# A decode block on one core: bias columns inside the rows of the first load, and the first load as four loads of stepped partitions

## The chip, the core and the metric

The kernel runs on one core of a Trainium2 chip. The metric is the device time of one execution in microseconds (us). Before the change it is 1050.35 us, the median of three runs from 1050.26 to 1050.51.

## What is computed

One token goes through a transformer block whose two layer norms are shifted, scaled and gated by six vectors that come from a condition `c`: attention of 32 heads over a cache of 8192 positions of 192 elements, and then a dense layer with a squared ReLU. All data are 32-bit floats. Cut to what matters, the reference is:

```python
def reference(A_x, A_k_cache, A_v_cache, A_wq, A_wo, B_x, B_w1, B_b1, B_w2, B_b2, c, w_mod):
    def _A_ref(x, k_cache, v_cache, wq, wo):      # H, Sk, Dh = 32, 8192, 192; D = 640
        q = (x @ wq).reshape(B, Sq, H, Dh).transpose(0, 2, 1, 3)
        scores = jnp.einsum("bhqd,bhkd->bhqk", q, k_cache) * (Dh ** -0.5)
        p = _softmax(scores, axis=-1)
        o = jnp.einsum("bhqk,bhkd->bhqd", p, v_cache)
        return o.transpose(0, 2, 1, 3).reshape(B, Sq, H * Dh) @ wo

    def _B_ref(x, w1, b1, w2, b2):                # F = 1536
        h = x @ w1 + b1
        r = jnp.where(h > 0, h, 0)
        return (r * r) @ w2 + b2

    x = A_x                                       # 1 x 1 x 640
    mod = (_silu(c) @ w_mod).reshape(c.shape[0], 6, 1, -1)
    sa, ca, ga, sb, cb, gb = (mod[:, i] for i in range(6))
    h = _layernorm(x) * (1 + ca) + sa
    x = x + ga * _A_ref(h, A_k_cache, A_v_cache, A_wq, A_wo)
    h = _layernorm(x) * (1 + cb) + sb
    return x + gb * _B_ref(h, B_w1, B_b1, B_w2, B_b2)
```

The caches alone are 2 x 32 x 8192 x 192 x 4 bytes = 403 MB, and each byte is used once.

## The kernel before

**How it is written.** `Program` records the instructions of every engine in the order in which `block_kernel` calls them, works out which semaphores each has to wait for, and `write` (line 139) then emits each engine's stream. So nearly every instruction has line 167 in the profile, and one tells them apart by engine and tile. Waits are found from the ranges of partitions and columns that instructions read and write: `extent` (line 207) gives the range, `overlap` (219) says whether two ranges meet, `within` (223) whether one covers the other. Each load from DRAM (`dma_start` to on-chip memory) takes one of eight semaphores in turn, and waits until the load eight places earlier has landed (lines 104 to 109).

**Loads.** All loads are issued by SP (`nc.sync`), in the order in which they are called. They go into three large buffers called `slot` (line 240) that are used in turn; a load waits until the last readers of its buffer are done. The first buffer takes `first_t`: for each of 128 partitions, a row of `WM` columns of the modulation weights, `WQ` columns of the first query weights, and `VEC` columns of `c` and `x` (33,320 bytes in all). Line 244 loads it in one piece. Then come the K block of head 0 (k0, line 350) and in the loop over heads (line 476) the V block of head 0 (v0), the four small loads of the bias vectors into a tile `bbc` of its own (lines 485 to 488, cut into 8, 4, 12 and 104 partitions by `BB_CUT`), and from then on a K and a V block for each head in turn. `kx` rows also carry slices of the query and output weights for later heads. k1 goes into the buffer of `first_t`, v1 into that of k0, and so on. After the last head SP loads the weights of the dense part (lines 517 to 531).

**The start.** ACT and DVE compute silu of `c` (lines 352 to 356); DVE weighs the modulation weights (`weigh`, line 334) while the layer norm of `x` runs beside it; TensorE sums over partitions and then forms the first two heads' query (`query`, line 371, called at 381). Then `spread` (line 293) turns the columns of `x` into rows: ACT copies each column 32 times into a tile `spread`, of which there is one buffer, and DVE transposes that to `x_t` (line 382). The biases get the same treatment at head 3 (line 490), into `bbt`; `bbt` is used only in the dense part (lines 569 and 581).

**One head.** `keys` (line 386) multiplies the K block with the query on DVE, and sums over the 192 elements on DVE, with GpSimd adding halves of some. `softmax` and `values` follow; TensorE multiplies with the V block. The query of the next pair of heads is formed from the tail of a K row.

Of the kernel before, what the change touches and what calls it, by code (L numbers as in the profile page):

```python
# [1 line left out]

# [9 lines left out]
P = 128  # L12
D = 640
# [7 lines left out]
KB = DG // 32  # L21
FB = FG // 32
# [5 lines left out]
WQ = KB * PW  # L28
ROW = KV + WO
WM = KB * 2 * D  # L30
VEC = 2 * KB
DA = 128
DB = DH - DA
REP = 8
# [2 lines left out]
WO_AT = {2 * i + 4: i for i in range(-1, NPAIR - 2)} | {H - 1: NPAIR - 2}  # L37
WQ_AT = {2 * i + 1: i + 1 for i in range(NPAIR - 1)}
WIDE = {h for h, i in (WO_AT | WQ_AT).items() if i >= 0}
BB_CUT = (8, 4, 12, 104)  # L40
HALF = DG // 2
W2_CUT = (0, 6 * D, 9 * D, 11 * D, 11 * D + G * HALF, FB * D)
EPS = 1e-5
# [7 lines left out]
class Program:  # L51
# [43 lines left out]
    def record(self, engine, name, args, kwargs):  # L95
# [14 lines left out]
        else:  # L110
            self.ticks[engine] += 1
            mark = (engine, self.ticks[engine])
        places = [(extent(a), w) for a, w in [(a, False) for a in reads] + [(a, True) for a in writes] if a.space != MemoryType.DRAM]
        for place, write in places:
            for other, who, wrote in self.uses.get(place[0], ()):
# [91 lines left out]
def extent(ap):  # L207
    row = ap.tensor.shape[1]
    (step, n), *free = ap.ap
    p, lo = divmod(ap.offset, row)  # L210
    hi = lo + sum((c - 1) * s for s, c in free) + 1
    end = p + (n - 1) * (step // row) + 1
    bank = ap.space == MemoryType.PSUM
    if bank:
        p, end, lo, hi = p // 32 * 32, -(-end // 32) * 32, lo // 512 * 512, -(-hi // 512) * 512
    return ap.tensor.name, p, end, lo, hi, bank


def overlap(a, b):
    return a[1] < b[2] and b[1] < a[2] and a[3] < b[4] and b[3] < a[4]  # L220


def within(a, b):
    return b[1] <= a[1] and a[2] <= b[2] and b[3] <= a[3] and a[4] <= b[4]


def block_kernel(nc, first, kx, vx, wm1, w1, w2, bb, out):
    def const(shape, name):
        return nc.tile(shape, name)

    def work(shape, tag, bufs=2):
        return nc.tile(shape, tag, bufs)
# [6 lines left out]
    def slot():  # L239
        return nc.tile([P, ROW], "slot", 3, align=512)  # L240

    k_t, v_t = {}, {}
    first_t = slot()
    nc.sync.dma_start(first_t[:, :WM + WQ + VEC], first)

    ident = const([P, P], "ident")
    make_identity(nc, ident)
# [12 lines left out]
                            axis=AX.X, op=ALU.add)  # L260
# [3 lines left out]
                            axis=AX.X, op=ALU.add)  # L264
# [5 lines left out]

    vec = first_t[:, WM + WQ:WM + WQ + VEC]
    c_c = vec[:, :KB]
    x_c = vec[:, KB:2 * KB]
    bbc = const([P, FB + KB], "bbc")

    def load_k(h):
        k_t[h] = slot()
        n = K_PARTS.get(h, 1)
        cuts = [KV * c // n for c in range(n)] + [ROW if h in WIDE else KV]
        for a, b in zip(cuts, cuts[1:]):  # L280
            nc.sync.dma_start(k_t[h][:, a:b], kx[h, :, a:b])

    def load_v(h):
        v_t[h] = slot()
        nc.sync.dma_start(v_t[h][:, :KV], vx[h])
# [7 lines left out]
    def spread(src, n, name):  # L293

        t = work([P, FB + KB, 32], "spread", 1)
        nc.scalar.copy(t[:, :n], src[:, :, None].to_broadcast([P, n, 32]))
        r = const([P, 32 * n], name)
        nc.vector.transpose(r, t[:, :n].rearrange("p b r -> p (b r)"))
        return r

    def total(src, name):

        ps = psum("sm")
        n = src.shape[1]
        nc.tensor.matmul(ps[:, :n], ones, src, start=True, stop=True)
        return ps[:, :n]
# [35 lines left out]
    def attend(i, w, oT):  # L342

        nc.fresh = True
        for j in range(3):
            for g in range(G):
                nc.tensor.matmul(att[32 * g:32 * (g + 1), :DG], oT[:, j:j + 1].to_broadcast([P, 32]),
                                 w[:, j, DG * g:DG * (g + 1)], start=False, stop=(i == NPAIR - 1 and j == 2))
# [24 lines left out]
    def query(i, w):  # L373
        w = w.rearrange("p (b n) -> p b n", b=KB)
        ps = psum("q", at=0)
        for b in range(KB):
            nc.tensor.matmul(ps[:, :PW], h1[:, b:b + 1].to_broadcast([P, P]), w[:, b], start=(b == 0), stop=(b == KB - 1))
        qb_t[i] = work([P, PW], "qb")
        nc.scalar.activation(qb_t[i], ps[:, :PW], AF.Copy, scale=DH ** -0.5)

    query(0, first_t[:, WM:WM + WQ])
    x_t = spread(x_c, KB, "x_t")

    ri_t, o_t, sp_t, os_t, sum_t, m_t, pt_t = {}, {}, {}, {}, {}, {}, {}

    def keys(h, between):

        q = qb_t[h // 2][:, DH * (h % 2):DH * (h % 2 + 1)]
        sc = work([P, NPOS], "sc")
        t = k_t[h][:, :KV].rearrange("p (i d) -> p i d", d=DH)  # L390
        sums = SUMS.get(h, ((32, 0),))
        n = NPOS // len(sums)
        for c, (nf, na) in enumerate(sums):
            a, b = n - nf - na, n - na
            pr = t[:, c * n:(c + 1) * n]
            s = sc[:, c * n:(c + 1) * n]
            nc.vector.tensor_mul(pr, pr, q[:, None, :].to_broadcast([P, n, DH]))
            nc.gpsimd.tensor_add(pr[:, a:b, :DH // 2], pr[:, a:b, :DH // 2], pr[:, a:b, DH // 2:])
            for i in range(b, n):
                jk = work([P, DH], "jk")  # L400
                nc.scalar.activation(jk, pr[:, i], AF.Copy, accum_out=s[:, i:i + 1])
            nc.vector.tensor_reduce(s[:, :a], pr[:, :a], axis=AX.X, op=ALU.add)
            if c == 0:
                between()
            nc.vector.tensor_reduce(s[:, a:b], pr[:, a:b, :DH // 2], axis=AX.X, op=ALU.add)
        return sc

    def softmax(h, sc):
        mp = work([P, 1], "mp")
        nc.vector.tensor_reduce(mp, sc, axis=AX.X, op=ALU.max)  # L410
        ps = psum("sm")
        nc.tensor.transpose(ps[:, :P], mp.to_broadcast([P, P]), ident)
        nm = work([P, 1], "nm")
        nc.vector.tensor_reduce(nm, ps[:, :P], axis=AX.X, op=ALU.max, negate=True)

        p = work([P, NPOS, REP], "p", 1)
        i = h // 2
        if h % 2 == 0:
            sp_t[i] = work([P, 2], "sp", 3)
        nc.scalar.activation(p, sc[:, :, None].to_broadcast([P, NPOS, REP]), AF.Exp, bias=nm,  # L420
                             accum_out=sp_t[i][:, h % 2:h % 2 + 1])
        return p
# [17 lines left out]
    def own(h, after=None):  # L440

        i, a = h // 2, h % 2
        if not a:
            m_t[i] = work([P, 2, 1024], "own", 1)
            os_t[i] = work([P, P], "os", 3).rearrange("p (a d) -> p a d", a=2)
        if i not in ri_t and (a or i == NPAIR - 1):
            ri_t[i] = work([P, 2], "ri", 3)
            nc.vector.reciprocal(ri_t[i], sum_t.pop(i))
        m, o = m_t[i][:, a], o_t.pop(h)
        cuts = (0, 512, 1024) if h == H - 1 else (0, 1024)  # L450
        for lo, hi in zip(cuts, cuts[1:]):
            nc.vector.tensor_mul(m[:, lo:hi], o[:, lo:hi], mask[:, lo:hi], after=after)
        if i == NPAIR - 1:
            nc.vector.tensor_reduce(os_t[i][:, a], m[:, 512:].rearrange("p (j d) -> p d j", d=DB), axis=AX.X, op=ALU.add)
        elif a:
            nc.vector.tensor_reduce(os_t[i], m_t[i][:, :, 512:].rearrange("p a (j d) -> p a d j", d=DB), axis=AX.X, op=ALU.add)
# [19 lines left out]
    for h in range(H):  # L476
        i = h // 2
        if h % TURN == 1 and (h < H - 1 or nc.turns):
            nc.loop(h < H - 1)
        if h:  # L480
            load_k(h)
        load_v(h)
        if h == 0:
            nc.gpsimd.memset(v_t[0][:, KV:ROW], 0.0)
            r0 = 0
            for n in BB_CUT:
                nc.sync.dma_start(bbc[r0:r0 + n], bb[r0:r0 + n])
                r0 += n
        if h == 3:
            bbt = spread(bbc, FB + KB, "bbt")  # L490

        def wo():
            if h in WO_AT:
                attend(WO_AT[h], k_t[h][:, KV:ROW].rearrange("p (j n) -> p j n", j=3), oT_t.pop(WO_AT[h]))

        def between():
            if h in WQ_AT:
                query(WQ_AT[h], k_t[h][:, KV:ROW])
            if h < H - 1:
                wo()  # L500

        sc = keys(h, between)
        p = softmax(h, sc)
        if h == H - 1:
            sum_t[i] = total(sp_t.pop(i), f"sum{i}")
            wo()
        if h:
            own(h - 1, qb_t.get(h // 2 + 1))
        if h % 2 == 0 and h:
            turn(i - 1)  # L510
        if h == H - 1:
            turn(i, (0,))
        values(h, p)
        if h % 2 and h < H - 1:
            sum_t[i] = total(sp_t.pop(i), f"sum{i}")
# [132 lines left out]
```

## Time and profile before

| | before |
|---|---|
| median of 3 runs | 1050.35 us (1050.26 to 1050.51) |
| the profiled execution | 1050.38 us |
| its span, first to last instruction | 1049.1 us |
| read from DRAM | 451.82 MB, 431 GB/s over the span |
| DVE busy | 829.3 us (79%) |
| PE busy | 457.0 us (44%) |
| POOL busy | 213.3 us (20%) |
| ACT busy | 69.0 us (7%) |
| load queue, share of 16 DMA engines | 99.6% |

PE is TensorE, DVE is VectorE, ACT is ScalarE, POOL is GpSimd, and SP issues the loads. Busy time of an engine is the sum of its instructions; the DMA share is the busy share of the core's 16 DMA engines. The span is what the profiler saw of the execution; the device time holds a little more around it.

### The profile page before, as it was taken

The numbers are of one execution on the slowest core, as the hardware profiler recorded it, in microseconds if no ns is written. First come the engines' busy times: TensorE is split into PE (matmuls) and PEld (weight loads), VectorE is DVE, ScalarE is ACT, GpSimd is POOL, SyncE is SP. The second block draws the span as 40 slices with busy tenths as digits, with TensorE's granted clock in tenths as the row PEclk, the third lists the DMA queues.
The fourth block names the chain that finished last, engine by engine and source line by source line (L and its number), as shares of the span: only waits on it lengthen the run. The fifth ranks groups of instructions, "written<-read, shape, count | busy, mean of one in ns | idle before, by whom it ended". The sixth has DMA issues, their size and how long they took to land. (4 is left out here: it accounts for less than half of the span.)

```text
span 1049.1 us, 6398 instructions
## 1 busy us (share of the span) xinstructions
PE 457.0 (44%) x2736; PEld 207.5 (20%) x2736; DVE 829.3 (79%) x284; ACT 69.0 (7%) x247; POOL 213.3 (20%) x50
## 2 busy tenths in 40 slices
PE   1153452535445064453526355163443516353456
PEld 0011221112122031222203122121212103121223
DVE  6788778988787987878888787897878798778852
ACT  1000000000000000000000000000000000012330
POOL 1221122221122221022222022222012222022100
PEclk9666665766657576675666658566665766666569
DMA  9999999999999999999999999999999999999998
GB/s 403 446 429 430 419 448 433 422 448 431 430 427 437 445 424 440 435 435 429 428 446 431 431 426 444 437 427 437 437 430 427 435 444 433 428 440 435 428 424 357
DMA packets 11266, 451.99 MB, mean 431 GB/s; under 512 B 1525, under 2 KB 1781, under 8 KB 2037
## 3 DMA queue, kind: packets, MB, share of 16 engines
q1 hardware_dynamic: 11253, 451.83, 99.6%
q8 instruction: 7, 0.11, 0.0%
q14 instruction: 6, 0.05, 0.0%
HBM read 451.82 MB, written 0.00 MB: 431 GB/s over the span
## 5 line engine op out<-in xcount | busy, mean ns | idle before, releaser
L167 DVE TENSOR_TENSOR slot<-slot,qb 128x12288 f32<-128x12288 f32 (+2 forms) x37 | 415.3, 11225 | 133.3 <-DMA slot<-in_kx 133.3
L167 POOL TENSOR_TENSOR slot<-slot 128x3072 f32<-128x3072 f32 (+2 forms) x37 | 210.3, 5683 | 791.6 <-DVE slot L167 791.6
L167 DVE TENSOR_REDUCE sc<-slot 128x32 f32<-128x6144 f32 (+5 forms) x74 | 307.0, 4150 | 13.3 <-POOL slot L167 12.0
L167 PE MATMUL ps_o<-slot,p 128*32 128x512 f32 x1536 | 240.8, 791 | 22.2 <-PEq L161 21.0
L167 PE MATMUL ps_q<-slot,ln_h 128*128 128x384 f32 x160 | 88.9, 728 | 80.6 <-PEq L161 79.3
L167 PE MATMUL ps_sm<-ident,mp 128*128 128x128 f32 x32 | 14.0, 438 | 248.9 <-PEq L161 213.0
L167 PEld LDWEIGHTS ps_o<-slot,p 128*32 128x32 f32 x1536 | 63.4, 140 | 175.3 <-issue 171.6
L167 PE MATMUL ps_q<-slot,oT 128*32 128x160 f32 x408 | 29.5, 453 | 154.6 <-PEq L161 154.4
L167 PEld LDWEIGHTS ps_q<-slot,ln_h 128*128 128x128 f32 x160 | 45.4, 296 | 128.5 <-issue 122.7
L167 PEld LDWEIGHTS ps_sm<-ident,mp 128*128 128x128 f32 x32 | 5.7, 179 | 267.3 <-issue 229.9
L167 ACT ACTIVATE p<-sc,nm 128x512 f32<-128x512 f32 x32 | 23.1, 721 | 525.7 <-DVE nm L167 525.7
L167 PE MATMUL ps_sm<-ri,own 128*128 128x1 f32 x256 | 56.5, 350 | 0.0
L167 PEld LDWEIGHTS ps_sm<-ri,own 128*128 128x128 f32 x256 | 55.0, 326 | 0.2
L167 PEld LDWEIGHTS ps_q<-slot,oT 128*32 128x32 f32 x408 | 18.2, 158 | 158.1 <-issue 155.2
L167 DVE TENSOR_TENSOR own<-ps_o,mask 128x1024 f32<-128x1024 f32 (+1 forms) x33 | 38.9, 1178 | 9.5 <-PE ps_o L167 9.5
L167 DVE TENSOR_REDUCE os<-own 128x128 f32<-128x1024 f32 (+1 forms) x17 | 30.2, 1774 | 0.6
L167 PE MATMUL ps_sm<-ri,os 128*64 128x1 f32 x64 | 6.4, 247 | 55.1 <-POOLq L165 54.4
L167 DVE TENSOR_REDUCE nm<-ps_sm 128x1 f32<-128x128 f32 x32 | 9.3, 292 | 21.2 <-PE ps_sm L167 21.2
L167 ACT ACTIVATE jk<-slot 128x192 f32<-128x192 f32 x69 | 24.0, 349 | 32.0 <-DVE slot L167 32.0
L167 ACT ACTIVATE qb<-ps_q 128x384 f32<-128x384 f32 x16 | 7.8, 490 | 272.8 <-PE ps_q L167 272.8
L167 PEld LDWEIGHTS ps_sm<-ri,os 128*64 128x64 f32 x64 | 5.3, 203 | 60.4 <-issue 58.4
L167 ACT ACTIVATION_READ_ACCUMULATOR jk<-slot 128x1 f32 x69 | 12.9, 187 | 0.0
(81 smaller groups left out, 93.4 us busy)
## 6 DMA issues: line engine op xcount, KB each, us to landing
slot<-in_kx SPq DMA_DIRECT2D x28, 7104.0 KB, 28.1
slot<-in_vx SPq DMA_DIRECT2D x32, 6144.0 KB, 22.6
slot<-in_kx SPq DMA_DIRECT2D x2, 6144.0 KB, 25.4
slot<-in_kx SPq DMA_DIRECT2D x2, 4032.0 KB, 23.8
slot<-in_kx SPq DMA_DIRECT2D x2, 3072.0 KB, 16.9
slot<-in_first SPq DMA_DIRECT2D x1, 4165.0 KB, 12.5
slot<-in_wm SPq DMA_DIRECT2D x1, 3840.0 KB, 25.5
slot<-in_w SPq DMA_DIRECT2D x1, 3840.0 KB, 31.8
```

The lines of the kernel that those rows point to most:

```text
L167: i = getattr(engine, name)(*args, **kwargs)
```

## The change

The bias columns are put into the rows of `first`, behind `c` and `x`: `VEC` grows from 10 to 27 columns, the array `bb`, its tile and its four loads go, and `bbc` becomes a view of `first_t`. The spread of the biases to `bbt` is called right after that of `x`, ahead of the first head, and no longer at head 3. The first load is issued as four: partitions 0, 8, 16, .. (16 of them), then 4, 12, 20, .. (16), then 2, 6, 10, .. (32), then the odd ones (64). So that these loads don't wait for each other, `extent` also gives the step of the partitions, `overlap` uses it (two ranges meet only if their starts agree modulo the common divisor of the steps), and `within` holds only where the covering range has no step.

```diff
-VEC = 2 * KB
+VEC = 3 * KB + FB
+FIRST_CUT = ((0, 8), (4, 8), (2, 4), (1, 2))
...
-BB_CUT = (8, 4, 12, 104)
...
-    return ap.tensor.name, p, end, lo, hi, bank
+    return ap.tensor.name, p, end, lo, hi, bank, 1 if bank else max(step // row, 1)
 
 
 def overlap(a, b):
-    return a[1] < b[2] and b[1] < a[2] and a[3] < b[4] and b[3] < a[4]
+    return a[1] < b[2] and b[1] < a[2] and a[3] < b[4] and b[3] < a[4] and (a[1] - b[1]) % gcd(a[6], b[6]) == 0
 
 
 def within(a, b):
-    return b[1] <= a[1] and a[2] <= b[2] and b[3] <= a[3] and a[4] <= b[4]
+    return b[6] == 1 and b[1] <= a[1] and a[2] <= b[2] and b[3] <= a[3] and a[4] <= b[4]
...
-    nc.sync.dma_start(first_t[:, :WM + WQ + VEC], first)
+    for r, step in FIRST_CUT:
+        nc.sync.dma_start(first_t[r::step, :WM + WQ + VEC], first[r::step])
...
-    bbc = const([P, FB + KB], "bbc")
+    bbc = vec[:, 2 * KB:]
...
     x_t = spread(x_c, KB, "x_t")
+    bbt = spread(bbc, FB + KB, "bbt")
...
-            r0 = 0
-            for n in BB_CUT:
-                nc.sync.dma_start(bbc[r0:r0 + n], bb[r0:r0 + n])
-                r0 += n
-        if h == 3:
-            bbt = spread(bbc, FB + KB, "bbt")
...
-        "first": np.concatenate([rows(wm[:, :2 * D], KB), wq[0], column(c, KB), column(a(A_x).ravel()[order], KB)], axis=1),
+        "first": np.concatenate([rows(wm[:, :2 * D], KB), wq[0], column(c, KB), column(a(A_x).ravel()[order], KB),
+                                 column(B_b1, FB), column(a(B_b2)[order], KB)], axis=1),
...
-        "bb": np.concatenate([column(B_b1, FB), column(a(B_b2)[order], KB)], axis=1),
```

## Rows read from the trace of the kernel before

**Rows 1.** The page: span, busy time, DMA over the run, load queue, HBM.

```profile
span 1049.1 us, 6398 instructions
PE 457.0 (44%) x2736; PEld 207.5 (20%) x2736; DVE 829.3 (79%) x284; ACT 69.0 (7%) x247; POOL 213.3 (20%) x50
...
DMA  9999999999999999999999999999999999999998
...
q1 hardware_dynamic: 11253, 451.83, 99.6%
...
HBM read 451.82 MB, written 0.00 MB: 431 GB/s over the span
```

**Rows 2.** Windows view, middle of the run; columns in the first line.

```profile
core 0: us, PE busy (x) PEld busy (x) DVE busy (x) ACT busy (x) POOL busy (x), PEclk, DMA share, GB/s
13.00:1000.00 987.00, 426.09 (x2381) 191.92 (x2381) 804.57 (x249) 58.86 (x208) 208.41 (x36) 0.65 1.00 434
```

**Rows 3.** Chain that ended last, its end: start us, us, what.

```profile
1020.41 25.14 DMA slot<-in_w
1045.55 0.04 issue
1045.59 1.17 PE ps_q L167 x32
```

**Rows 4.** Windows view, start of the stream and start of k1's rows.

```profile
0.00:1.70 1.70, 0.00 (x0) 0.00 (x0) 0.00 (x0) 0.97 (x1) 0.85 (x7) 1.00 0.00 0
1.70:2.60 0.90, 0.00 (x0) 0.00 (x0) 0.52 (x1) 0.31 (x1) 0.84 (x6) 1.00 1.76 444
2.60:3.60 1.00, 0.00 (x0) 0.00 (x0) 1.00 (x1) 0.00 (x0) 1.00 (x1) 1.00 0.35 133
3.60:4.60 1.00, 0.00 (x0) 0.00 (x0) 1.00 (x1) 0.00 (x0) 0.36 (x1) 1.00 1.24 533
12.30:13.00 0.70, 0.00 (x0) 0.00 (x0) 0.00 (x0) 0.00 (x0) 0.00 (x0) 1.00 2.61 1124
41.30:42.10 0.80, 0.00 (x0) 0.00 (x0) 0.80 (x1) 0.00 (x0) 0.00 (x0) 0.50 2.78 1148
```

**Rows 5.** Timeline of SP, first issues: start us, us, what.

```profile
0.74 0.38 SPq L167 DMA_DIRECT2D slot<-in_first  x1
1.18 0.42 SPq L167 DMA_DIRECT2D slot<-in_kx  x1
1.65 0.42 SPq L167 DMA_DIRECT2D slot<-in_vx  x1
2.11 1.77 SPq L167 DMA_DIRECT2D bbc<-in_bb  x4
31.24 0.36 SPq L167 DMA_DIRECT2D slot<-in_kx  x1
```

**Rows 6.** DMA view of the window 41.30:42.10.

```profile
DMA packets 197, 0.92 MB, mean 1148 GB/s; under 512 B 181, under 2 KB 181, under 8 KB 181
```

**Rows 7.** The page, DMA issues: count, KB each, us from issue to landing.

```profile
slot<-in_first SPq DMA_DIRECT2D x1, 4165.0 KB, 12.5
```

**Rows 8.** Timeline about head 3: the bias spread.

```profile
119.77 0.64 ACT L167 COPY spread<-bbc 128x544 f32<-128x544 f32 x1
120.45 0.74 DVE L167 STREAM_TRANSPOSE bbt<-spread 128x544 f32<-128x544 f32 x1 [4.93 <-ACT spread L167]
```

**Rows 9.** Timeline of the first two heads.

```profile
30.90 0.32 ACT L167 COPY spread<-slot 128x160 f32<-128x160 f32 x1
31.23 1.28 ACT L167 ACT_TABLE_LOAD   x1
...
31.25 0.35 DVE L167 STREAM_TRANSPOSE x_t<-spread 128x160 f32<-128x160 f32 x1 [6.82 <-ACT spread L167]
31.51 12.92 DVE L167 TENSOR_TENSOR slot<-slot,qb 128x12288 f32<-128x12288 f32 x1
...
54.61 0.35 SPq L167 DMA_DIRECT2D slot<-in_vx  x1
...
59.11 12.96 DVE L167 TENSOR_TENSOR slot<-slot,qb 128x12288 f32<-128x12288 f32 x1 [3.42 <-DMA slot<-in_kx]
```

**Rows 10.** Windows view, before and at the start of v1's rows.

```profile
57.30:58.10 0.80, 0.80 (x8) 0.20 (x4) 0.00 (x0) 0.00 (x0) 0.00 (x0) 0.50 0.00 0
58.10:58.90 0.80, 0.80 (x8) 0.20 (x4) 0.00 (x0) 0.00 (x0) 0.00 (x0) 0.50 2.28 983
```

**Rows 11.** Windows view, end of the stream.

```profile
1043.00:1044.00 1.00, 0.63 (x20) 0.30 (x11) 0.00 (x0) 0.00 (x0) 0.00 (x0) 1.00 0.99 401
1044.00:1045.00 1.00, 1.00 (x24) 0.68 (x24) 0.00 (x0) 0.00 (x0) 0.00 (x0) 1.00 0.69 270
1045.00:1046.00 1.00, 0.43 (x16) 0.40 (x16) 0.00 (x0) 0.00 (x0) 0.00 (x0) 1.00 0.45 159
```

More of the change, by code (lines that the diff above doesn't have):

```diff
@@ L1 @@
-from math import prod
+from math import gcd, prod
 from concourse import mybir
@@ L215, in extent, with block_kernel @@
         p, end, lo, hi = p // 32 * 32, -(-end // 32) * 32, lo // 512 * 512, -(-hi // 512) * 512
-    return ap.tensor.name, p, end, lo, hi, bank
+    return ap.tensor.name, p, end, lo, hi, bank, 1 if bank else max(step // row, 1)
 def overlap(a, b):
-    return a[1] < b[2] and b[1] < a[2] and a[3] < b[4] and b[3] < a[4]
+    return a[1] < b[2] and b[1] < a[2] and a[3] < b[4] and b[3] < a[4] and (a[1] - b[1]) % gcd(a[6], b[6]) == 0
 def within(a, b):
-    return b[1] <= a[1] and a[2] <= b[2] and b[3] <= a[3] and a[4] <= b[4]
-def block_kernel(nc, first, kx, vx, wm1, w1, w2, bb, out):
+    return b[6] == 1 and b[1] <= a[1] and a[2] <= b[2] and b[3] <= a[3] and a[4] <= b[4]
+def block_kernel(nc, first, kx, vx, wm1, w1, w2, out):
     def const(shape, name):
```

## Prediction

> **What bounds the kernel now.** I read the page first, then the chain of work that ended last, then windows of the run, and then the first 60 us as a timeline. On the page the reader is to see that the load queue is busy for 99.6% of the span, that the DMA row stands at 9 in all slices but the last, and that 452 MB come in at 431 GB/s [rows 1]. VectorE is busy for 79% of the span and waits again and again for the next K block; no compute engine is the bound. The window over 987 us in the middle gives a DMA share of 1.00 at 434 GB/s [rows 2], that is 434/16 = 27.1 GB/s for each of 16 DMA engines. The chain that ended last says the same of the end: 25.14 us of it is the last weight loads, and behind them come 1.17 us of matmul, the small VectorE work on `y` and the store, issued at 1047.57 of a span of 1049.1 [rows 3]. So the time is: 1.7 us until the first packet moves (no DMA in 0.00:1.70 [rows 4]), the stream until about 1046, and some 3 us of tail. A change at the head counts in full if it delays or shortens the stream, and for nothing if it only moves compute in front of a load that is waited for anyway.
>
> **The base of the sum.** The profiled execution took 1050.38 us for a span of 1049.1, so 1.3 us lie around the span; it is 0.03 above the median of 1050.35. The sum starts from 1050.38.
>
> **The bias loads go.** Four loads of 0.3 to 6.9 KB are removed. On SP they cost 1.77 us from 2.11 on [rows 5], and SP's next instruction, the load of k1, then waits until 31.24 for the first buffer; so their issue time costs nothing. In the stream they lie between v0 and k1. All 181 packets under 512 B that start in 41.30:42.10 (128 bias rows, the rest semaphore writes) fit into that 0.8 us, in which k1's first rows start as well [rows 6, 4]. If the small ones took the whole window the gain would be 0.8 us; the window also holds 0.91 MB in packets that start there, so the engines were not held up for that long. I take -0.1, bounds -0.8 and 0. The same bytes now ride in the first load, 68 B more on a row of 33,320: 0.2% of 9.8 us, +0.02.
>
> **Three more issues at the head.** The first load was one issue of 0.38 us; k0's and v0's followed at 1.18 and 1.65 [rows 5]. Four issues of about 0.44 us move k0's to about 2.5. What hides that is the first load itself: k0's rows start in 12.30:13.00 (1124 GB/s for 0.7 us are 787 KB, 16 rows of 49,152 B; the view books a packet where it starts [rows 4]). Cover left: over 8 us. Cost 0; without the cover it would be 1.3 us. Nothing else is on SP between them. The first stepped load gives each engine one row of 1.23 us, and the next issue comes 0.44 us later, so no engine runs dry between the four. Three more sets of semaphore writes: +0.03, by the same small packets.
>
> **The start of the stream.** In 1.70:2.60 there start 0.9 us x 444 GB/s = 400 KB, 12 rows; in 2.60:3.60 133 KB, 4 rows; in 3.60:4.60 533 KB, 16 rows [rows 4]. So twelve engines begin about 1.0 us after the issue at 0.74 and four about 0.9 us later. A load of 16 rows may let the four start with the rest: at most -0.9. But all sixteen start their second row within the same 1 us, so the four made most of it up already. I take -0.1, bounds -0.9 and 0.
>
> **The rate of the stepped loads** is the term that decides, and no row shows it. 4165 KB [rows 7] are 4.265 MB; at 434 GB/s that is 9.83 us, 1.23 us for each of an engine's 8 rows. One bound is that they run like the first load of before, the nearest row: +0. The other is that a step of 8 partitions sends the engines two and two to one place of the on-chip memory while other places stand idle; each row then takes twice as long: +9.83. Every large load of the kernel covers all 128 partitions in one piece, and those that don't are the bias loads of 8.5 KB together, whose rate can't be read. I take +0 because the nearest row, the same bytes from the same array to the same tile, runs at full rate; the other end stays in the range. [...]
>
> **The bias spread moves from head 3 to the start.** It is an ACT copy of 0.64 us and a DVE transpose of 0.74 [rows 8]. Both spreads share one buffer, so the copy waits for the transpose of `x_t`, which ends at 31.60, and the large multiply of k0 behind it on DVE starts not at 31.51 [rows 9] but at 31.60 + 0.03 + 0.64 + 0.03 + 0.74 = 33.04: +1.53 on DVE's path. SP's k1 load, which waits for the last reader of the first buffer, moves from 31.24 to about 32.3; v0 runs until 41.3, so 8 us of cover hide it. Tighter is v1: its load was issued at 54.61 [rows 9], when k0 was used up, and goes to 56.14. Its first packets then come 1.0 us later, or 1.9 for the slow four: 57.1 to 58.1. No packet starts in 57.30:58.10, and sixteen rows start in 58.10:58.90 [rows 10]: the engines turn to v1 only after 58.1, since k1 lasts until then. So the move just fits, with 0 to 1.0 us left. I take +0. Upper bound: if ACT's table load of 1.28 us [rows 9] came between the two copies, v1's packets would be 0.2 to 1.2 us late, +1.2. Behind that the delay dies: DVE waited 3.42 us for k1 at 59.11 [rows 9]. At head 3 DVE no longer sits 4.93 us [rows 8] before the transpose; what comes next there is again a wait for a load, so that is worth 0.
>
> **Sum:** 1050.38 - 0.1 + 0.02 + 0.03 - 0.1 = 1050.2.
>
> **The end of the stream** adds scatter. The DMA share falls over 1043 to 1046 as 0.99, 0.69, 0.45 [rows 11]: the engines finish over some 2 us, and the last one sets the time. The bias loads were cut in four unequal pieces, so they weigh unevenly on the engines, and a new start shifts them too; 0.31 + 0.55 = 0.86 us is what perfect balance would gain. I allow 0.8 down and 0.8 up.
>
> **Rivals.** (A) *The stepped loads run at half rate throughout.* Two engines that share a place finish together and meet again at the next row, all 8 rows long. Price 8 x 1.23 = 9.8 us, all of it on the stream: 1060.0. For it: the stream's rate is the same over 987 us, for arrays with different row lengths in DRAM, so the limit sits behind the source, in the engine or at the place where it writes. Against it: if the limit is the engine's own, the order of partitions is nothing to it. It decides from the first row on which two engines meet. (B) *Only part of it.* If just the two loads of 16 rows meet, that is 2 x 1.23 = 2.5 us, 1052.7; if one of each pair gets ahead by a row and they no longer meet, 1.2 us, 1051.4. (C) *v1 comes late*, in the place of the hidden spread: up to +1.2, 1051.4; against it the 0 to 1.0 us that are left. (D) *Faster in earnest.* Over 2.1 us would need more than the whole 1.7 us ahead of the first packet. (E) *The four loads do not start the late engines earlier*, so that the change does only the moves that are hidden: 1050.3, within the forecast.
>
> **How the numbers follow.** A measurement of this kernel can tell about 0.2%, 2.1 us, from no change. Forecast 1050.2, with (C) and (E), own range 1049.4 to 1051.4: chance 0.54. (A), 1058.5 to 1061: 0.30. (B), 1051.4 to 1055: 0.14, of which a little over half is beyond 2.1 us. (D): 0.02. So faster 0.02, same 0.60, slower 0.38. To hold 8 in 10 the range has to reach into (A): 1049.4 to 1060.5.
>
> **What would show it.** In the windows at the head, the stepped loads right at full rate: sixteen rows start by 2.6, k0's rows start by 12.3 to 13.0 again, and ACT's first work on `c` stands near 13.3. Under (A) k0 starts near 22 and ACT near 23; under (B) near 14 to 15 and 15 to 16. The multiply of k0 should start 1.5 us later behind the first landing than before, 19.8 instead of 18.3 us behind it, and a window just ahead of v1's first rows should show a DMA share that does not sag; if it sags, (C). The DMA share in the middle stays 1.00. I am wrong if the stream's length from the first packet to 1046 changes by more than 1 us though the head windows look like before.

## The result and the profile after

The changed kernel takes 1054.36 us, the median of six runs from 1054.14 to 1054.85. Against the runs of the kernel before it is slower by a factor of 1.0037, with a 95% interval of 1.0027 to 1.0047. That is 4.0 us more, where 1050.2 had been forecast.

The page of the changed kernel shows the stream as full as before, only longer:

```profile
span 1053.0 us, 6394 instructions
...
DMA  9999999999999999999999999999999999999998
...
q1 hardware_dynamic: 11136, 451.83, 99.5%
...
HBM read 451.82 MB, written 0.00 MB: 429 GB/s over the span
```

The end of the chain that ended last (start us, us, what) has the same steps with nearly the same lengths (the last matmuls 1.21 us in place of 1.17). They start at 1049.51 in place of 1045.59 [rows 3], so all 3.9 us are lost ahead of the tail:

```profile
1049.46 0.04 issue
1049.51 1.21 PE ps_q L167 x32
1050.72 0.02 issue
```

Where they are lost is seen in windows of the changed kernel (last two columns: share of the DMA engines and GB/s; a packet's bytes are booked where it starts, so GB/s times the length, divided by the row, counts the rows that start):

```profile
core 0: us, PE busy (x) PEld busy (x) DVE busy (x) ACT busy (x) POOL busy (x), PEclk, DMA share, GB/s
1.70:2.60 0.90, 0.00 (x0) 0.00 (x0) 0.52 (x1) 0.00 (x0) 0.84 (x6) 1.00 2.51 556
2.60:3.60 1.00, 0.00 (x0) 0.00 (x0) 1.00 (x1) 0.00 (x0) 1.00 (x1) 1.00 0.13 33
3.60:6.40 2.80, 0.56 (x8) 0.23 (x8) 2.80 (x2) 0.00 (x0) 0.36 (x1) 1.00 0.86 191
8.30:14.50 6.20, 0.00 (x0) 0.00 (x0) 0.87 (x1) 0.00 (x0) 0.00 (x0) 1.00 1.00 431
14.50:15.30 0.80, 0.00 (x0) 0.00 (x0) 0.00 (x0) 0.00 (x0) 0.00 (x0) 1.00 2.28 983
...
60.30:61.20 0.90, 0.00 (x0) 0.00 (x0) 0.29 (x1) 0.57 (x1) 0.00 (x0) 0.50 2.30 710
61.20:61.90 0.70, 0.41 (x4) 0.20 (x8) 0.45 (x1) 0.24 (x2) 0.00 (x0) 0.50 0.64 211
```

**The first loss, 2.3 us.** By 2.60, 15 rows of 33,388 B have started and one more by 3.60. Then 16 rows (535 KB) start from 3.60 to 6.40, and the third set only after that: the engine that is first through its two rows needs 4.3 us for them, from 2.1 on. By the trace's packet records the rows of the two loads of 16 partitions take 2.39 and 2.40 us in the mean, the next ones 1.63, and all that follow 1.24 (8.30 to 14.50 runs at 431 GB/s). The first row of each engine was slow before the change too: 1.93 us in the mean, and 1.24 or less from the second on. So, in means over the sixteen engines, the loss is 0.23 us from the later first packets, 0.45 and 1.16 from the two loads of 16, and 0.39 from the third set. Sixteen rows of k0 start in 14.50:15.30, where they started in 12.30:13.00 before [rows 4].

**The second loss, 1.6 us.** v1's sixteen first rows started together in 58.10:58.90 before [rows 10]. Moved by the first loss they would start between 60.3 and 61.1. Thirteen do so by 61.20 and three only in 61.20:61.90. The stretch from k1's first row to k2's first row holds the same bytes in both kernels, 435 GB/s over 31.2 us and 423 over 32.1. The windows view of the kernel before:

```profile
41.40:72.60 31.20, 7.95 (x50) 2.25 (x51) 26.90 (x7) 0.81 (x2) 7.13 (x2) 0.61 1.01 435
```

The same view of the changed kernel, its stretch 0.9 us longer:

```profile
43.50:75.60 32.10, 9.38 (x51) 2.75 (x52) 30.36 (x7) 0.81 (x2) 7.79 (x2) 0.61 1.00 423
```

That is 0.9 us for the first engine; for the last one, by the packet records, v1's rows end at 77.2 in place of 73.3, 3.9 us later, so 1.6 us behind the first loss of 2.3. The slowest engine sets the end of the stream, and the 3.9 us are found again at the last matmuls. In the profiled executions of all eleven changed versions, the last of v1's rows and the whole span are late by the same time to 0.2 us, but for `e9_packed_source` (2.63 and 2.98) and `e1_bias_only` (1.73 and 2.37).

The packet records also show what this loss consists of. Ahead of v1's first rows the engines stand idle for 0.26 us in the mean; these rows then take 2.51 us in the mean, where they took 1.81 before. So most of the loss is in slow first rows, and the idle time is the smaller part.

Why v1 was late is seen in the timelines (start us, us, what, idle time ahead and its releaser). In the kernel before, ACT has loaded its table ahead of its wait for the first load:

```profile
0.73 1.28 ACT L167 ACT_TABLE_LOAD   x1 [0.73 <-PEq L640]
13.30 0.21 ACT L167 ACTIVATE silu<-slot 128x5 f32<-128x5 f32 x1 [11.29 <-DMA slot<-in_first]
```

In the changed kernel it does so behind that wait:

```profile
0.73 2.52 SPq L167 DMA_DIRECT2D slot<-in_first  x4
...
15.87 1.28 ACT L167 ACT_TABLE_LOAD   x1 [15.87 <-DMA slot<-in_first]
17.17 0.21 ACT L167 ACTIVATE silu<-slot 128x5 f32<-128x5 f32 x1
...
34.69 0.34 DVE L167 STREAM_TRANSPOSE x_t<-spread 128x160 f32<-128x160 f32 x1 [6.39 <-ACT spread L167]
35.07 0.64 ACT L167 COPY spread<-slot 128x544 f32<-128x544 f32 x1 [0.41 <-DVE x_t L167]
...
35.74 0.74 DVE L167 STREAM_TRANSPOSE bbt<-spread 128x544 f32<-128x544 f32 x1 [0.71 <-ACT spread L167]
36.41 12.92 DVE L167 TENSOR_TENSOR slot<-slot,qb 128x12288 f32<-128x12288 f32 x1
...
59.51 0.33 SPq L167 DMA_DIRECT2D slot<-in_vx  x1
```

k0's multiply starts 4.90 us later than before (36.41 and 31.51 [rows 9]), and so does the issue of v1 (59.51 and 54.61). The stream itself was only 2.3 us late. The 4.90 us are: the landing of the first load, at which ACT leaves its wait (15.87 in place of 13.30, +2.57); a table load of ACT that now stands behind that wait (+1.30); the bias spread behind that of `x` (+1.46: from the start of the transpose to `x_t` to k0's multiply it is 1.72 us in place of 0.26); less 0.42 us, by which the query's matmuls were shorter (5.57 us in place of 5.99).

### The profile page after: what moved, and what is told of

Its sections match the earlier page's. It is cut to its first block, busy times and chain, and to the rows that moved or that the text cites. A ratio compares the mean times of both kernels' runs of the same rounds, so it can differ in the third digit from the quotient of the medians.

```text
span 1053.0 us, 6394 instructions
## 1 busy us (share of the span) xinstructions
PE 458.9 (44%) x2736; PEld 208.3 (20%) x2736; DVE 829.3 (79%) x284; ACT 69.0 (7%) x247; POOL 213.3 (20%) x50
```

## Experiments

**The theory** after the comparison: two separate losses. The two loads of 16 partitions run at half rate (2.39 and 2.40 us a row, where 1.24 is the full rate); the loads of 32 and 64 do not (1.63 us, then 1.24). And what piles up ahead of k0's multiply (late landing, table load, bias spread) makes v1 late. That two engines each meet at one place of the on-chip memory in the loads of 16 is a supposition; the traces show times alone. **The rivals:** all of the loss is in the stepped loads; the first rows are slow because the stream starts with small loads, or because there are four of them; the step is slow on DRAM's side. All medians stand against 1050.44 to 1050.46 of the kernel before on the same chips.

### One part at a time

`e1_bias_only`, the changed kernel with the first load in one piece:

```diff
-    for r, step in FIRST_CUT:
-        nc.sync.dma_start(first_t[r::step, :WM + WQ + VEC], first[r::step])
+    nc.sync.dma_start(first_t[:, :WM + WQ + VEC], first)
```

> The bias columns ride in the rows of the first load, which is one load again; the bias spread stays ahead of head 0. Theory: the 4 us of the change are two pieces, about 2.3 us from the stepped loads of 16 partitions (their rows take 2.40 us in place of 1.23) and about 1.6 us from v1's load, which comes late because the bias spread, a table load of ACT and the late landing pile up ahead of k0's multiply. With one load the landing is at 13.2 again and the table load ahead of it, so only the spread's 1.5 us are left ahead of v1's issue (56.1 in place of 54.6), v1's packets come between 57.1 and 58.2, just in time: 1050.3, between 1050.0 and 1050.9. Rival (the spread alone makes v1 late): a gap of 1 us and more ahead of v1's rows, 1051.4 to 1052.

Measured: 1050.77 (ratio 1.0006, 0.9997 to 1.0016), but runs from 1050.3 to 1053.7. So this version stands on the edge that the prediction had worked out, with 0 to 1.0 us left for v1. The profiled execution took 1052.76 and fell over it: v1 was issued at 56.83, and of its sixteen first rows 12 (655 GB/s for 0.9 us) start by 58.90 and 4 only in the next 1.2 us:

```profile
58.00:58.90 0.90, 0.09 (x4) 0.09 (x8) 0.00 (x0) 0.76 (x2) 0.00 (x0) 0.50 1.88 655
58.90:60.10 1.20, 1.20 (x8) 0.32 (x12) 0.75 (x1) 0.00 (x0) 0.00 (x0) 0.50 0.53 164
```

`e2_steps_only`, the four stepped loads, with the bias in its own loads again and spread at head 3:

```diff
-VEC = 3 * KB + FB
+VEC = 2 * KB
...
-    bbt = spread(bbc, FB + KB, "bbt")
...
+        if h == 3:
+            bbt = spread(bbc, FB + KB, "bbt")
```

> The first load as four stepped loads, but the bias in its own four loads and spread at head 3, as in the kernel before. Theory: the stream is 2.3 us late from k0 on; k0's multiply starts 2.6 + 1.3 us later (late landing, table load behind it), so v1's issue is at about 58.5 and its packets at 59.5 to 60.4, as the engines run out of k1 at about 60.4: at most a small gap, 1052.7, between 1052.4 and 1053.3. Rival (all of the loss is in the stepped loads, the gap at v1 is a by-product): 1054.3.

Measured: 1052.90 (1.0023, 1.0014 to 1.0033), as the theory said. The steps alone cost 2.5 us and the bias alone 0.3, together 2.8 of the 4.0: by the medians the two parts hurt each other by 1.2 us. Each ratio's interval is about 1 us to either side, so the 0.3 can't be told from nothing, and the 1.2 is rough.

### What is slow about the stepped loads

`e3_reversed`, the same four loads in reverse order:

```diff
-FIRST_CUT = ((0, 8), (4, 8), (2, 4), (1, 2))
+FIRST_CUT = ((1, 2), (2, 4), (4, 8), (0, 8))
```

> The changed kernel with the four stepped loads in reverse order: the odd partitions (64), then 2, 6, .. (32), then 4, 12, .. (16), then 0, 8, .. (16). Theory (two engines meet at one place of the on-chip memory in a load of 16 stepped partitions): six rows of 1.24 us first, then two of 2.40; the windows show a full rate up to about 9 us and about half of it (16 rows in 2.4 us, some 220 GB/s) in the 4.8 us ahead of k0, which starts near 14.5; total as the changed kernel within 0.5 us, 1053.8 to 1054.8. Rival (the first rows are slow because the stream starts with small loads, whichever partitions they hold): full rate at the end, k0 near 12.6, and 1052 to 1052.5.

Measured: 1055.56 (four runs, 1055.19 to 1056.16). The slow rows moved to the end with the two loads of 16, so they are not slow because they stand at the start of the stream. (The very first rows are slow here too, 1.86 us in the mean, as in the kernel before.) Windows of this kernel:

```profile
2.00:10.10 8.10, 0.76 (x8) 0.23 (x8) 7.09 (x2) 0.00 (x0) 1.96 (x6) 1.00 1.00 396
10.10:14.30 4.20, 0.00 (x0) 0.00 (x0) 0.00 (x0) 0.00 (x0) 0.00 (x0) 1.00 1.07 254
```

The last 32 rows (254 GB/s x 4.2 us = 1.07 MB) take 4.2 us; by the packet records they take 2.10 and 2.39 us each. The total is 0.8 us above the range given: here the landing, and with it v1's issue (61.38), are later still than in the changed kernel, while k0's first row starts at about the same time (14.4), so the gap at v1 is wider: by the packet records the engines stand idle ahead of it for 1.39 us in the mean, in place of 0.26.

`e4_four_of_32`, as many loads, but of 32 partitions:

```diff
-FIRST_CUT = ((0, 8), (4, 8), (2, 4), (1, 2))
+FIRST_CUT = ((0, 4), (1, 4), (2, 4), (3, 4))
```

> The changed kernel with four stepped loads of 32 partitions each (step 4, starting at 0, 1, 2, 3): as many issues and semaphores, no load of 16. Theory: no row takes 2.4 us, k0's rows start near 12.7 (the stepped issue takes 0.2 us longer), so 1.9 us of the 2.3 come back; what is left is the gap at v1, since table load and spread are still ahead of k0's multiply: 1052.4, between 1052.0 and 1052.9. Rival (four pieces in place of one cost it, whatever their rows): k0 again near 14.6 and 1054.3.

Measured: 1052.25 (1.0016, 1.0007 to 1.0026), as the theory said. k0's sixteen first rows start in 12.60:13.20 (1311 GB/s), so four stepped loads without one of 16 cost the stream 0.3 us:

```profile
2.00:12.60 10.60, 0.76 (x8) 0.23 (x8) 7.08 (x2) 0.00 (x0) 1.96 (x6) 1.00 1.01 403
12.60:13.20 0.60, 0.00 (x0) 0.00 (x0) 0.00 (x0) 0.00 (x0) 0.00 (x0) 1.00 3.04 1311
```

`e6_contiguous`, as many rows in each load as the change has, without a step:

```diff
-    for r, step in FIRST_CUT:
-        nc.sync.dma_start(first_t[r::step, :WM + WQ + VEC], first[r::step])
+    for lo, hi in ((0, 16), (16, 32), (32, 64), (64, 128)):
+        nc.sync.dma_start(first_t[lo:hi, :WM + WQ + VEC], first[lo:hi])
```

> The changed kernel with the first load cut into partitions 0 to 15, 16 to 31, 32 to 63 and 64 to 127, no step. Theory (a load gets only the share of the write places that its partitions reach, and neighbours lie in one place): four engines meet in the first two loads, two in the others; rows of 4.9, 4.9, 2 x 2.45 and 4 x 2.45 us, the first load takes some 24.5 us in place of 9.9, and the total is 1050.4 + 14.7 + up to 2 for a late v1: 1065 to 1067. Rival (it is the step that costs, in the load's description or in DRAM): rows of 1.24 us, and 1052.3 as with four loads of 32.

Measured: 1065.93 (two runs). Neighbouring partitions are far worse than stepped ones, so the step itself is not the cause. The first load takes until 25.9, at 177 GB/s; k0's first rows start only then:

```profile
1.70:25.90 24.20, 0.76 (x8) 0.23 (x8) 7.09 (x2) 0.00 (x0) 2.21 (x6) 1.00 1.01 177
25.90:26.60 0.70, 0.00 (x0) 0.00 (x0) 0.00 (x0) 0.00 (x0) 0.00 (x0) 1.00 3.26 1124
```

The theory fits in the sum: its counts and the 1.23 us of a row gave 24.5 us, and from the first packet at 1.7 it measured 24.2. How many engines meet was assumed; the packet records show times alone. The single rows fit less well than the sum: 3.74 and 4.55 us in the mean for the two loads of 16, where 4.9 had been expected, and 2.47 to 3.17 for the other six sets, where 2.45 had been. This run also answers a rival of its own: a load of 16 has just one row for each of the 16 engines, in steps of 8 as well as here, and the rows differ all the same (2.40 and 4.55 us). So the set of partitions counts, and not only the small number of rows. A third set of 16 partitions, neither in steps of 8 nor neighbours, was not run.

`e9_packed_source`, the array `first` laid out in DRAM in the order in which the four loads take its rows, so that only the destination is stepped:

```diff
+    lo = 0
...
-        nc.sync.dma_start(first_t[r::step, :WM + WQ + VEC], first[r::step])
+        nc.sync.dma_start(first_t[r::step, :WM + WQ + VEC], first[lo:lo + P // step])
+        lo += P // step
...
```

> The changed kernel with the rows of the first array in the order in which the four loads take them, so that each load reads one packed piece of DRAM and only the destination is stepped. Theory (the destination decides): rows of the first two loads at 2.40 us as before, 1053.8 to 1054.9. Rival (the stepped read of DRAM is slow): full rate, k0 near 12.7, 1052.3.

Measured: 1053.45 (five runs), a little below the range given and far above the rival's. The rows of the two loads of 16 stay slow: 32 rows (248 GB/s x 4.3 us) start by 6.30, and the rest runs at 438:

```profile
2.00:6.30 4.30, 0.46 (x8) 0.23 (x8) 4.21 (x2) 0.00 (x0) 1.96 (x6) 1.00 1.04 248
8.20:14.30 6.10, 0.00 (x0) 0.00 (x0) 1.00 (x1) 0.00 (x0) 0.00 (x0) 1.00 1.02 438
```

So the stepped read is not what makes the rows slow; what is left is the destination. Here the landing came 0.6 us earlier than in the changed kernel, and the gap at v1 was narrower; whether the packed read is behind that, five runs don't settle.

### The late v1

`e5_early_table`, one Exp of one column on ACT ahead of its wait for the first load:

```diff
     nc.gpsimd.memset(eps_t, EPS)
+    nc.scalar.activation(const([P, 1], "warm_exp"), eps_t, AF.Exp)
```

> The changed kernel with one small Exp on ACT ahead of its wait for the first load, so that ACT's table load is done at the start and not behind the landing. Theory: everything on the way to v1's issue moves 1.3 us up, v1's issue to 58.2, its packets to 59.2 to 60.4; the engines run out of k1 from 60.3 on, so the gap all but closes and 1.0 to 1.6 of the 4.0 us come back: 1053.0, between 1052.6 and 1053.4. Rival (the gap at v1 costs nothing of its own): 1054.3.

Measured: 1052.86 (1.0029, 1.0018 to 1.0039). 1.5 of the 4.0 us come back by moving a table load that is not on the stream at all: v1 is issued at 58.32, and five of nine runs lie at 1052.6 to 1052.9; single ones reach 1055.5. That this version is on the edge again would explain them, but no trace shows such a run.

`e8_after_spread_first`, both spreads ahead of the first query:

```diff
+    x_t = spread(x_c, KB, "x_t")
+    bbt = spread(bbc, FB + KB, "bbt")
     query(0, first_t[:, WM:WM + WQ])
-    x_t = spread(x_c, KB, "x_t")
-    bbt = spread(bbc, FB + KB, "bbt")
```

> The changed kernel with both spreads ahead of the first query and not behind it, where DVE waits for TensorE anyway. Theory: k0's multiply starts at about 34.5 in place of 36.4, v1's issue goes to 57.6, its packets to 58.6 to 59.9, ahead of the end of k1 at 60.3; the gap closes and the loss is that of the stepped loads alone: 1052.6, between 1052.4 and 1053.0. Rival (the gap at v1 has another cause than the chain on DVE): 1054.3.

Measured: 1052.76 (1.0024, 1.0014 to 1.0033). v1 is issued at 57.79, its sixteen first rows start together in 60.60:61.20 (1311 GB/s for 0.6 us), and the stretch from k1 to k2 is back at 435 GB/s. What is left, 2.3 us, is the price of the stepped loads:

```profile
60.60:61.20 0.60, 0.60 (x8) 0.20 (x4) 0.00 (x0) 0.00 (x0) 0.00 (x0) 0.50 3.04 1311
...
43.90:75.10 31.20, 8.14 (x50) 2.40 (x51) 27.73 (x7) 0.81 (x2) 7.29 (x2) 0.61 1.00 435
```

The packet records of all these runs show how early is early enough. Count from the issue of v1 to the moment when the first engine is through with k1, and compare v1's sixteen first rows with the 1.81 us that they take undisturbed:

| v1 issued ahead by | kernels | first rows above 1.9 us | mean of the sixteen |
|---|---|---|---|
| 2.9 to 3.6 us | before, `e7_spread_first`, `e8_after_spread_first` | 0 | 1.81 us |
| 2.1 to 2.4 us | `e2_steps_only`, `e5_early_table`, `e10_four_of_32_spread_first` | 2 or 3 | 1.93 to 1.96 us |
| 1.8 us | `e6_contiguous` | 9 | 2.05 us |
| 1.2 to 1.4 us | `e1_bias_only`, `e9_packed_source` | 14 or 16 | 2.15 to 2.33 us |
| 0.8 us or less, in `e3_reversed` too late by 0.4 | the change, `e3_reversed`, `e4_four_of_32` | 15 or 16 | 2.51 to 2.62 us |

So v1 begins to cost when it is issued 2.1 to 2.4 us before the first engine is through with k1. Each row of the table is one profiled execution per kernel, and no run changed this lead alone; why the rows are slow is not shown.

### Without either loss

`e10_four_of_32_spread_first` joins the cuts of `e4_four_of_32` with the order of `e8_after_spread_first`.

> Four loads of 32 partitions (step 4) and both spreads ahead of the first query: neither rows at half rate nor a late v1. Theory: only the later first packet of a stepped issue is left, 0.3 to 0.4 us: 1050.8, between 1050.5 and 1051.1. Rival (four pieces have a further cost of their own): 1051.5 and more.

Measured: 1050.81 (1.0006, 0.9997 to 1.0015), as the theory said for the median; three of ten runs, at 1051.6, 1052.7 and 1052.8, lie where the rival put them (1051.5 and more). The first of the three is the profiled execution. Its packet records put the loss at v1 and not in the four pieces: v1 is issued 2.4 us ahead, two of its sixteen first rows take 3.17 and 2.64 us in place of 1.81, and the last of its rows ends 1.19 us later than before, where the whole execution is 1.23 us longer. The other two runs have no trace.

`e7_spread_first` is the bias in the rows, one first load (as `e1_bias_only`), and both spreads ahead of the query.

> The bias columns in the rows of the first load, that load in one piece, and both spreads ahead of the first query: what is left of the change without its two costs. Theory: the stream starts and runs as before, k0's multiply starts at about 31.1 and v1's load is issued ahead of 54.6, so v1 is never late and the scatter of the version with the spread behind the query (1050.3 to 1053.7) is gone; removing the bias loads is worth at most 0.1: 1050.3, between 1050.1 and 1050.6. Rival (the scatter of that version came from something else in the longer rows): again single runs above 1051.5.

Measured: 1050.46 (11 runs, 1050.25 to 1050.78), against 1050.46 of the kernel before: ratio 1.0000, 0.9991 to 1.0009. The scatter of `e1_bias_only` is gone, since v1 is issued at 54.40 and k0's multiply starts at 31.25. No version beat the kernel before; removing four small loads from a full stream is worth nothing that can be measured.

## Why the prediction was wrong

The forecast was no change, 1050.2. It came out slower by 4.0 us, inside the range (1049.4 to 1060.5), which reached that far only because of rivals (A) and (B).

- **What bounds the kernel**: right. The stream stayed the bound, and a loss at the head came out at the end in full: k0 is 2.3 us late, v1's last engine 3.9, the last matmuls 3.9. But the DMA share doesn't show such a loss: a slow row counts as busy. It was 1.00 over the stretch from k1 to k2 at 423 GB/s, and 1.01 in `e6_contiguous` at 177; the rate and the packets show it.
- **The rate of the stepped loads**: this step failed. It was put at +0, because the nearest row, the one load of before, runs at full rate. It measured 2.3 us. The first case of rival (B) came true: of the loads just the two of 16 run at half rate, priced at 2.5 us. That price is near in part by luck. It takes 1.23 us more for each of two rows; the two cost 0.45 and 1.16, since the first row took 1.93 us before as well and not 1.23, and a later start and the third set brought the rest. (A), half rate for all eight rows, did not come true. No run shows that two engines share a place, the supposition behind the +9.83 and both prices; what the runs showed in its place is times: 2.39 and 2.40 us a row in the two loads of 16, 1.63 in the next set and 1.24 in all that follow. `e4_four_of_32` shows that loads of 32 stepped partitions run at full rate (403 GB/s over 2.00:12.60, where the one load of before had 402 over 1.70:12.30), and in `e6_contiguous` the same 128 rows, in pieces of neighbours, took 24.2 us. The nearest row was near in bytes and array, but not in what mattered, the set of partitions of one load.
- **The bias spread**: the mechanism and its place were named, and its +1.53 us on DVE were right in size (1.46 in the changed kernel). It was put at 0 because 0 to 1.0 us were left. `e1_bias_only` shows that this margin is real and thin: a median 0.3 us up, and single runs 3 us up. The step failed because the other moves were not added to it: the landing and the stream were taken to move together, and the landing moved 2.57 us while k0's rows moved 2.3. ACT's table load was not expected ahead of silu at all. The margin itself was read too wide as well: it was counted to v1's first packet, and from 56.14 to the first end of k1 at 58.17 are 2.0 us, where runs with 2.1 us have two or three slow first rows. So rival (C), held at +1.2 at most and inside the forecast, cost 1.6 us on top of the first loss.
- **The table load**: missed. Before, ACT waits for one semaphore, and the table load of 1.28 us lies at 0.73 us ahead of the wait. Four loads mean four semaphores, and the wait shows up ahead of the table load, at 15.87. It is so in all eight kernels with four loads that leave the start of ACT alone (13.59 to 27.56 us), and in none of the three with one load (0.73 us); what puts the table load there is not shown. The prediction did see a table load near the spreads and gave it 1.28 us; it looked at the wrong one.
- **Three more issues**: the cover was right, the size was not. Four issues took 2.52 us, 0.63 each, and not 0.44. k0's issue at 3.30 was still early enough by 11 us.
- **The start of the stream**: -0.1 was taken. Fifteen of sixteen rows do start by 2.60, as hoped for, but by the packet records the first one comes at 2.12 and not at 1.74, and the sixteen start 0.23 us later in the mean, so nothing is gained.
- **The bias loads**: -0.1 was taken; `e7_spread_first` shows no gain that can be measured.

## What to carry to other kernels

When a load is cut by partitions, look at each piece by itself: a piece of 16 rows, stepped by 8, took 2.40 us a row and one of 16 neighbours up to 4.55, where 1.24 is the full rate, though all pieces together cover the same partitions as one load that ran at full rate. In a stream that never pauses, the time between a buffer's release and the moment the engines run dry is a budget; list it for the first heads, where the chain is longest, and charge all moves of a change to it together, waits for several semaphores among them. The budget ends before the engines are idle: v1 lost nothing when it was issued 2.9 us ahead, and something at 2.4. A cost that is hidden with little to spare can show up as scatter of single runs before it shows up in the median, as in `e1_bias_only` (median 1050.77, runs from 1050.3 to 1053.7).

## What the runs showed of the hardware that was not expected

- Four issues to stepped partitions take SP 2.52 us, four to runs of neighbouring ones 1.91 (`e6_contiguous`), one to all partitions 0.38; the first packet follows at 2.12 us with a step and at 1.74 without. The step is not all of it: k0's issue, which has none, takes 0.58 to 0.59 us behind either four, and 0.42 behind one.
- v1's first rows are slow when it is issued late: they take 1.81 us when it is issued 2.9 us or more ahead, and 2.51 in the mean at 0.81 us. The first rows of the whole stream take 1.93 us in the kernel before, in place of 1.24.
- A load of 32 stepped partitions runs at full rate (k0 at 12.6 in `e4_four_of_32`), one of 32 neighbours does not, and neither does one of 64 neighbours: in `e6_contiguous` the packet records give rows of 2.5 to 3.2 us for the last six sets.
- ACT's table load lies ahead of a wait for one load and behind a wait for four: 0.73 us in the kernel before, `e1_bias_only` and `e7_spread_first`, and 15.87 us in the changed kernel.
